# Six second-layer accumulations of a gated mix kernel split into two row tiles of 64 rows

## The chip, the cores and the metric

The kernel runs on one core of a Trainium2 chip. Its engines are TensorE (PE: matrix products, with weight loads shown apart as PEld), VectorE (DVE), ScalarE (ACT), GpSimd (POOL) and SyncE (SP, which here issues nearly all DMAs). Each engine runs its own instructions strictly in the order in which the program lists them, and waits for others through semaphores. The metric is the device time of one execution in microseconds, the median of several runs.

## What is computed

Two branches are mixed with a gate. Branch A is a short causal filter on `k`, a product with `v`, a long causal convolution over 2048 positions and a product with `q`. Branch B is a two-layer perceptron on the same `q`. Cut to what matters:

```python
x = A_q                                             # 2048 x 512
g = sigmoid((x * gate_w).sum(-1, keepdims=True))
k_shift = sum(k_pad[:, t:t + S] * shift_k[:, 3 - t] for t in range(4))
kv = k_shift * v
y = irfft(rfft(kv, 4096) * rfft(ssm_k, 4096))[:, :S] + kv * ssm_D
a = q * y
h = maximum(x @ w1, 0)                              # 2048 x 1792
b = h @ w2                                          # 2048 x 512
out = g * a + (1 - g) * b
```

## The kernel before

**Precision.** Every operand of the perceptron is split into a high and a low part of type fp32r (names ending in h and l, such as `hh` and `hl` for the hidden activations, `w1h` and `w1l` for the second layer's weights), and each product is made as three matmuls: high times high, high times low, low times high. That is three matmuls of 128 x 128 weights by 512 columns in place of one.

**Second layer.** `mlp2(era, c, s)` (lines 398 to 432) makes 128 rows of the second layer. The hidden dimension has 14 blocks of 128; an era is half of them (blocks 0 to 6, then 7 to 13). A chunk `c` is 512 positions, and `s` is one of its four groups of 128. So one accumulation is 7 blocks times 3 matmuls, 21 in all, into one bank of PSUM (`bank`, line 278; there are eight banks, and the planner counts them as "cv"). In era 0 the bank is then copied to a tile `y` by ACT (`keep`, lines 414 to 421); in era 1 DVE adds the bank to that tile (`plus`, line 429), or, in the last chunk, the final instruction reads the bank directly (`finish`, line 677). Chunk 3 comes first in era 1 and chunk 0 last.

**Convolution.** It runs in three stages beside the perceptron, with DRAM between them. Stage 1 (`stage1`, lines 451 to 471) is made of 16 units, named s1h and s1x in the profile: eight matmuls each on tiles of 32 rows x 64 columns, into four banks, copied out by ACT and stored. Stage 2 (`conv_mid`) begins when all of stage 1 is stored; its units are f_h and f_x (64 rows x 32 columns, line 575) and, two groups later, iv (32 x 64, line 652). Stage 3 begins when all of stage 2 is stored. It loads the result (`br`), and `conv_end` (lines 687 to 732) runs the cy matmuls (64 x 32, line 727) in two groups of four units, each unit of eight matmuls into two banks. `after` and `finish` then combine, on DVE, for each of the 16 output tiles: `t` from cy, the gate and q (line 737), in the last chunk also `t` plus the kept half of the second layer (line 740), and the output tile `o` (line 677), which SP stores.

**What sets the order.** Nothing is ordered by hand around the change. `Plan.order` (lines 97 to 232) is a list scheduler that runs when the program is built: every operation has an engine, a planned duration, a rank, dependencies, and buffers it takes and gives back. A stage-1 unit has `pair` set. It is placed only together with another one, right after an operation that carries `soon` (`twin`, lines 113 to 121), or alone when it has been waiting for over 50 planned microseconds (`LONG`, line 815). Before the change, the last block of every second-layer accumulation carries `soon`. Tile operations carry `tiles=True`, and the planner adds `SWITCH` at each change between tiles and full matmuls.

Of the kernel before, what the change touches and what calls it, by code (L numbers as in the profile page):

```python
# [11 lines left out]
OP = mybir.AluOpType  # L12

S, D, DFF = 2048, 512, 1792
# [52 lines left out]
def _flat(r):  # L67
    for x in r if isinstance(r, tuple) else (r,):
        yield from _flat(x) if isinstance(x, tuple) else (x,)


class Plan:
# [5 lines left out]
    def add(self, eng, dur, rank, fn, deps=(), take=(), give=(), dma=0, fifo=(), tiles=False, port=False, alt=None, pair=0, soon=False, ends=False):  # L78
        rank = tuple(_flat(rank))
        op = dict(tiles=tiles, alt=alt, port=port or eng == "POOL" and not dma, eng=eng, dur=dur, rank=rank, fn=fn, take=tuple(take), give=tuple(give), dma=dma, fifo=tuple(fifo),  # L80
                  pair=pair, soon=soon, ends=ends or soon, wait=0, next=[], asked=0.0, n=len(self.ops), rest=(), member=False)
        op["fn"] = fn if alt is None else lambda: fn(op["eng"])
        for d in deps:
            if d is not None:
                d["next"].append(op)
                op["wait"] += 1
        for q in fifo:
            self.turn.setdefault(q, []).append(op["n"])
        self.ops.append(op)
        return op  # L90
# [144 lines left out]
def act_time(n, psum=False):  # L235
    return n * 0.000833 + (0.05 if psum else 0.093)


def dve_time(n):
    return n * 0.001042 + 0.12  # L240


MM = 0.227
# [5 lines left out]
def build(tc, wf, xp, qn, kn, vn, hn, dn, sh, gw, w1, w2, cs1, ccf, cci, cib, out):  # L249
    nc = tc.nc  # L250
# [18 lines left out]
    add = plan.add  # L269
    T = {}  # L270
    cpool = [None, None]

    def tile_of(key, tag, w=D, dt=F32, bufs=None, rows=P, p=None):
        nm = tag + "_" + "_".join(map(str, key[1:] if len(key) > 1 else key))
        T[key] = (p or cpool[0]).tile([rows, w], dt, tag=tag, bufs=bufs or room.get(tag, 1), name=nm)
        return T[key]

    def bank(key, tag="cv"):
        T[key] = pm.tile([P, D], F32, tag=tag, bufs=room0[tag], name="_".join(map(str, key)))
        return T[key]  # L280
# [3 lines left out]
    mm = nc.tensor.matmul  # L284
# [6 lines left out]
    xdone, wdone, xhigh = {}, {}, {}  # L291
    ERAS = [range(0, NF // 2), range(NF // 2, NF)]
    CHUNKS = [list(range(NCHUNK)), list(range(NCHUNK))[::-1]]
# [56 lines left out]
    hdone, m1last, m2 = {}, {}, {}  # L350
    ydone, ystore = {}, {}
    at = [0]
# [45 lines left out]
    def mlp2(era, c, s):  # L398
        at[0] += 1
        prev = None  # L400
        fs = ERAS[era]
        z = slice(s * P, (s + 1) * P)
        for f in fs:
            def go(f=f):
                ps = bank(("m2", era, c, s)) if f == fs[0] else T["m2", era, c, s]
                mm(ps, T["hh", era, c, f][:, z], T["w", "h", 1, f], start=f == fs[0], stop=False)  # L406
                mm(ps, T["hh", era, c, f][:, z], T["w", "l", 1, f], start=False, stop=False)  # L407
                mm(ps, T["hl", era, c, f][:, z], T["w", "h", 1, f], start=False, stop=f == fs[-1])  # L408

            prev = add("PE", 3 * MM, (1, at[0], f), go, [hdone[era, c, f], wdone[1, f], prev], ["cv"] if f == fs[0] else (),  # L410
                       (["hh"] if s == 3 else []) + (["w2"] if s == 3 and c == CHUNKS[era][-1] else []), soon=f == fs[-1])
        n, i = 4 * c + s, at[0]
        if era == 0:
            def keep():
                if c:
                    tile_of(("y", n), f"y{n}", p=mp)
                else:
                    if s % 2 == 0:
                        tile_of(("y2", n), "yr", 2 * D, p=mp)
                    T["y", n] = T["y2", n - s % 2][:, s % 2 * D:(s % 2 + 1) * D]  # L420
                nc.scalar.copy(T["y", n], T["m2", era, c, s])

            two = ["yr"] if c == 0 and s % 2 == 0 else []
            ydone[n] = add("ACT", act_time(D, True), (0, -900 + i), keep, [prev], two, ["cv"], fifo=two)
            if c == 0:
                ystore[n] = add("SP", ISSUE, -20 + s, lambda: nc.sync.dma_start(yd[:, n], T["y", n]), [ydone[n], ystore.get(n - s % 2)], (), ["yr"] if s % 2 else [], dma=ROW)
        elif c != CHUNKS[1][-1]:
            def plus():
                nc.vector.tensor_tensor(T["y", n], T["m2", era, c, s], T["y", n], op=OP.add)

            ydone[n] = add("DVE", dve_time(D), (0, -900 + i), plus, [prev, ydone[n]], (), ["cv"])
        m2[era, c, s] = prev
# [322 lines left out]
    w = add("PE", WARM * 2 * MM / 2, (-3,), warm, (), ["cv"], ["cv"])  # L755
# [10 lines left out]
    for era in range(2):  # L766
        for n, c in enumerate(CHUNKS[era]):
            if era == 0 and c == NCHUNK - 1:
                for i in range(2):
                    for f in ERAS[1]:  # L770
                        load_w(i, f, -50 + f + 10 * i)
            for f in ERAS[era]:
                if era == n == 0 and f < G:
                    if f == 0:
                        mlp1_first()
                    continue
                give = ["x"] * 4 if f == ERAS[era][-1] and not (era == 0 and c == NCHUNK - 1) else []
                if era == 0 and c == NCHUNK - 1 and f >= G - 1:
                    give += ["w1"] * (4 if f == G - 1 else 1)
                mlp1(era, c, f, give)  # L780
            if n + 1 < NCHUNK:
                for k in range(4):
                    load_x(era, CHUNKS[era][n + 1], k, -40)
            for s in range(4):
                mlp2(era, c, s)
# [105 lines left out]
```

## Time and profile before

| what | value |
|---|---|
| median of 3 runs | 385.6 us (385.55 to 386.24) |
| the profiled execution | 385.97 us |
| its span, first to last instruction | 384.2 us |
| PE busy | 99% of the span |
| DVE busy | 69% |
| ACT, POOL busy | 34%, 24% |
| granted TensorE clock | 0.999 |

The profile is one execution. Its own time is 1.8 us over its span; the median of the runs is 1.4 us over that span. A timeline row gives the start in us from the span's start, the duration in us, the engine, the line and operation, the tiles (output, then inputs, numbers left out) with the tile of the array in use (rows*columns), and a count where rows are merged; in brackets stands the idle time before it and what ended it. Matmuls overlap: a matmul is shown longer than the distance to the next one, so the distance between starts is what one costs.

### The profile page before, as it was taken

To read this page: it belongs to the slowest core of one execution; us is meant where nothing else is said; L and a number is where in the kernel's file an instruction comes from. 1 tells how busy PE (TensorE), PEld (TensorE's weight loads), DVE (VectorE), ACT (ScalarE), POOL (GpSimd) and SP (SyncE) were. 2 spreads that over 40 slices of the span, in tenths; PEclk is the share of its full clock that TensorE was granted. 3 is DMA by queue.
4 is the path that set the end of the run, shared out by engine and by line. 5 is a ranking of instruction groups with operands and counts; after the bars stand their busy time and mean duration, and the time that the engine had idled before them with its cause. 6 is when DMAs were issued, how large, how long until landed. Compare 5 with 4: busy or idle time off the path is not lost.

```text
span 384.2 us, 6567 instructions
## 1 busy us (share of the span) xinstructions
PE 379.8 (99%) x2505; PEld 273.8 (71%) x2505; DVE 266.7 (69%) x356; ACT 128.8 (34%) x242; POOL 91.5 (24%) x77
## 2 busy tenths in 40 slices
PE   9999999999999999999999999999999999999996
PEld 5888788668877788788655765565587788688684
DVE  4698999797989028114799687897872347687691
ACT  5643524573147525533224022313400333012100
POOL 0000000000000000000199968866995001000000
PEclk9999999999999999999999999999999999999999
DMA  7997893898648763589867876686460798399331
GB/s 274 368 317 255 298 351 113 293 333 323 208 121 330 295 234 109 185 296 275 285 203 238 307 265 227 241 308 232 139 204 3 241 342 320 120 325 357 117 124 56
DMA packets 43474, 92.51 MB, mean 241 GB/s; under 512 B 4625, under 2 KB 7201, under 8 KB 43442
## 3 DMA queue, kind: packets, MB, share of 16 engines
q1 hardware_dynamic: 43090, 91.77, 68.8%
q8 instruction: 20, 0.33, 0.4%
q10 hardware_dynamic: 288, 0.26, 0.2%
q14 instruction: 12, 0.10, 0.1%
q0 software_dynamic: 64, 0.05, 0.0%
HBM read 61.66 MB, written 30.41 MB: 240 GB/s over the span
## 4 chain that ended last, share of the span: by engine, by line
PE 99%; DVE 0%; DVEq 0%; issue 0%
PE m L406 14%; PE m L407 13%; PE m L408 13%; PE m L376 13%; PE m L377 12%; PE m L378 12%; PE iv L652 4%; PE f_h L575 4%; PE f_x L575 4%; PE m L362 3%; PE s1x L459 2%; PE s1h L459 2%; PE cy L727 2%; PE warm L753 1%; DVE o L677 0%; DVEq L887 0%
## 5 line engine op out<-in xcount | busy, mean ns | idle before, releaser
L623 POOL TENSOR_TENSOR p<-p,ha 128x512 f32<-128x512 f32 x32 | 41.1, 1308 | 202.2 <-DVE ha L617 201.6
L406 PE MATMUL m<-w1h_h,hh 128*128 128x512 f32 x224 | 88.7, 396 | 0.0
L407 PE MATMUL m<-w1l_l,hh 128*128 128x512 f32 x224 | 87.3, 390 | 0.0
L408 PE MATMUL m<-w1h_h,hl 128*128 128x512 f32 x224 | 87.2, 389 | 0.0
L389 ACT ACTIVATE hh<-m 128x512 fp32r<-128x512 f32 x56 | 33.1, 598 | 126.4 <-PE m L378 122.1
L392 DVE SCALAR_TENSOR_TENSOR hl<-m,hh 128x512 fp32r<-128x512 f32 x56 | 38.3, 688 | 44.5 <-ACT hh L389 44.3
L376 PE MATMUL m<-xh_h,w0h_h 128*128 128x512 f32 x160 | 63.0, 394 | 0.0
L377 PE MATMUL m<-xl_l,w0h_h 128*128 128x512 f32 x160 | 62.3, 390 | 0.0
L378 PE MATMUL m<-xh_h,w0l_l 128*128 128x512 f32 x160 | 62.3, 389 | 0.0
L406 PEld LDWEIGHTS m<-w1h_h,hh 128*128 128x128 f32 x224 | 42.0, 188 | 19.1 <-ACT ev L464 6.5
L408 PEld LDWEIGHTS m<-w1h_h,hl 128*128 128x128 f32 x224 | 42.0, 188 | 9.0
L407 PEld LDWEIGHTS m<-w1l_l,hh 128*128 128x128 f32 x224 | 42.1, 188 | 8.3
L376 PEld LDWEIGHTS m<-xh_h,w0h_h 128*128 128x128 f32 x160 | 30.0, 188 | 11.1 <-issue 4.2
L378 PEld LDWEIGHTS m<-xh_h,w0l_l 128*128 128x128 f32 x160 | 30.0, 188 | 6.4
L377 PEld LDWEIGHTS m<-xl_l,w0h_h 128*128 128x128 f32 x160 | 30.0, 188 | 6.0
L518 DVE TENSOR_TENSOR acc<-acc,tmp 128x1024 f32<-128x1024 f32 x24 | 29.3, 1222 | 0.6
L302 DVE TENSOR_TENSOR w1l_l<-raw,w1h_h 128x512 fp32r<-128x512 f32 x14 | 9.4, 686 | 17.7 <-ACT w1h_h L299 17.7
L662 ACT COPY bv<-iv 128x512 f32<-128x512 f32 x16 | 8.7, 589 | 37.1 <-PE iv L652 31.9
L515 DVE TENSOR_TENSOR tmp<-in,sht_sht 128x512 f32<-128x512 f32 x32 | 20.8, 685 | 0.1
L623 POOL TENSOR_TENSOR p<-p,qa 128x512 f32<-128x512 f32 x16 | 20.7, 1317 | 0.0
L617 DVE TENSOR_TENSOR ha<-f_x,ha 128x1024 f32<-128x1024 f32 x16 | 19.5, 1221 | 1.3 <-DVE qb L617 0.5
L623 POOL TENSOR_TENSOR p<-p,qb 128x512 f32<-128x512 f32 x16 | 20.3, 1290 | 0.0
(72 smaller groups left out, 468.1 us busy)
## 6 DMA issues: line engine op xcount, KB each, us to landing
sa<-ev SPq DMA_DIRECT2D x64, 256.0 KB, 3.0
sb<-bv SPq DMA_DIRECT2D x32, 256.0 KB, 3.4
br<-sb SPq DMA_DIRECT2D x16, 512.0 KB, 6.8
raw<-xp SPq DMA_DIRECT2D x28, 256.0 KB, 4.2
raw<-w SPq DMA_DIRECT2D x24, 256.0 KB, 3.8
r_x<-sa SPq DMA_DIRECT2D x12, 512.0 KB, 5.1
in<-kn SPq DMA_DIRECT2D x10, 512.0 KB, 5.0
r_h<-sa SPq DMA_DIRECT2D x10, 512.0 KB, 6.3
```

The source lines that it names most:

```text
L376: mm(ps, part("h", f, k), T["x", "h", xe, c, k], start=k == 0, stop=False)
L377: mm(ps, part("h", f, k), T["x", "l", xe, c, k], start=False, stop=False)
L378: mm(ps, part("l", f, k), T["x", "h", xe, c, k], start=False, stop=k == 3)
L389: nc.scalar.activation(tile_of(("hh", era, c, f), "hh", dt=F32R, p=mp, bufs=HB), T["m1", era, c, f], AF.Relu)
L392: nc.vector.scalar_tensor_tensor(tile_of(("hl", era, c, f), "hl", dt=F32R, p=mp, bufs=HB), T["m1", era, c, f], 0.0, T["hh", era, c, f].bit ...
L406: mm(ps, T["hh", era, c, f][:, z], T["w", "h", 1, f], start=f == fs[0], stop=False)
L407: mm(ps, T["hh", era, c, f][:, z], T["w", "l", 1, f], start=False, stop=False)
L408: mm(ps, T["hl", era, c, f][:, z], T["w", "h", 1, f], start=False, stop=f == fs[-1])
L515: nc.vector.tensor_tensor(o[:, z], T["k", c + (j == 0) + part][:, u], T["sht",][:, j * D:(j + 1) * D], op=OP.mult)
L518: nc.vector.tensor_tensor(T["acc", c], T["acc", c], T[dst], op=OP.add)
L575: mm(ps[b][32 * j:32 * j + 32, :], T[k("cf")][at, 64 * j + 32 * o:64 * j + 32 * o + 32], T[k("r", t, j // 2)][at, (j % 2) * D:(j % 2 + 1) ...
L623: nc.gpsimd.tensor_tensor(planes("p", dst, n), planes("p", dst, n), planes(src, u, n), op=OP.add if sign > 0 else OP.subtract)
```

## The change

In six accumulations (era 0, chunks 1 and 2, `s` of 0, 1 and 2), each of the 21 matmuls becomes two: one over rows 0 to 63 of the operands, one over rows 64 to 127. The two go to different row tiles of the array, and each has a bank of its own. ACT copies the first bank to `y` as before, and a new DVE instruction (`both`) adds the second bank to `y`. The planned duration of a block stays at three matmuls; the first block takes two banks; and the last block of such an accumulation no longer carries `soon`.

```diff
@@ mlp2
         fs = ERAS[era]
+        wide = era == 0 and c in (1, 2) and s < 3
         z = slice(s * P, (s + 1) * P)
         for f in fs:
             def go(f=f):
+                if wide:
+
+                    for i in range(2):
+                        ps = bank(("m2", era, c, s, i)) if f == fs[0] else T["m2", era, c, s, i]
+                        T["m2", era, c, s, i] = ps
+                    for n, (a, b) in enumerate((("hh", "h"), ("hh", "l"), ("hl", "h"))):
+                        for i in range(2):
+                            r = slice(64 * i, 64 * i + 64)
+                            mm(T["m2", era, c, s, i], T[a, era, c, f][r, z], T["w", b, 1, f][r, :], start=f == fs[0] and n == 0, stop=f == fs[-1] and n == 2)
+                    return
                 ps = bank(("m2", era, c, s)) if f == fs[0] else T["m2", era, c, s]
...
-            prev = add("PE", 3 * MM, (1, at[0], f), go, [hdone[era, c, f], wdone[1, f], prev], ["cv"] if f == fs[0] else (),
-                       (["hh"] if s == 3 else []) + (["w2"] if s == 3 and c == CHUNKS[era][-1] else []), soon=f == fs[-1])
+            prev = add("PE", 3 * MM, (1, at[0], f), go, [hdone[era, c, f], wdone[1, f], prev], ["cv"] * (1 + wide) if f == fs[0] else (),
+                       (["hh"] if s == 3 else []) + (["w2"] if s == 3 and c == CHUNKS[era][-1] else []), soon=f == fs[-1] and not wide)
...
-                nc.scalar.copy(T["y", n], T["m2", era, c, s])
+                nc.scalar.copy(T["y", n], T["m2", era, c, s, 0] if wide else T["m2", era, c, s])
+
+            def both():
+                nc.vector.tensor_tensor(T["y", n], T["m2", era, c, s, 1], T["y", n], op=OP.add)
...
             ydone[n] = add("ACT", act_time(D, True), (0, -900 + i), keep, [prev], two, ["cv"], fifo=two)
+            if wide:
+                ydone[n] = add("DVE", dve_time(D), (0, -900 + i), both, [ydone[n]], (), ["cv"])
```

The order of the whole program follows from the planner, so the change moves more than the six accumulations. In the rows below, a name such as m_0_2_0 is the bank of era 0, chunk 2, group 0 (a fourth number is the row tile), hh_2_1 the hidden activations of chunk 2, block 1, and w1h_h_1 the weights of block 1. From the changed lines on, line numbers are 11 higher in `mlp2`'s old matmuls (406 to 408 become 417 to 419) and 16 higher behind it (stage 1's 459 becomes 475, cy's 727 becomes 743, 677 becomes 693, 709 becomes 725, 714 becomes 730, 737 becomes 753, 740 becomes 756). The row-tile matmuls stand on line 414.

PE, in chunk 2's second-layer accumulations, before: two stage-1 units stand side by side at the boundary between two accumulations.

```order
L408 MATMUL m_0_2_0_1133<-w1h_h_6_353,hl_2_6_1151 128x512
L459 MATMUL s1x_0_1181<-acc_791,s1c_s1t 64x512 x2
L459 MATMUL s1x_1_1184<-acc_791,s1c_s1t 64x512 x2
L459 MATMUL s1x_2_1187<-acc_791,s1c_s1t 64x512 x2
L459 MATMUL s1x_3_1190<-acc_791,s1c_s1t 64x512 x2
L459 MATMUL s1h_0_1198<-in_681,s1c_s1t 64x512 x2
L459 MATMUL s1h_1_1201<-in_681,s1c_s1t 64x512 x2
L459 MATMUL s1h_2_1204<-in_681,s1c_s1t 64x512 x2
L459 MATMUL s1h_3_1207<-in_681,s1c_s1t 64x512 x2
L406 MATMUL m_0_2_1_1219<-w1h_h_0_237,hh_2_0_1006 128x512
```

PE at the same accumulation now: a single unit stands between two blocks of a split accumulation.

```order
L414 MATMUL m_0_2_0_0_1073<-w1h_h_1_244,hl_2_1_983 128x512
L414 MATMUL m_0_2_0_1_1074<-w1h_h_1_244,hl_2_1_983 128x512
L475 MATMUL s1h_0_1096<-in_573,s1c_s1t 64x512 x2
L475 MATMUL s1h_1_1099<-in_573,s1c_s1t 64x512 x2
L475 MATMUL s1h_2_1102<-in_573,s1c_s1t 64x512 x2
L475 MATMUL s1h_3_1105<-in_573,s1c_s1t 64x512 x2
L414 MATMUL m_0_2_0_0_1073<-w1h_h_2_277,hh_2_2_993 128x512
L414 MATMUL m_0_2_0_1_1074<-w1h_h_2_277,hh_2_2_993 128x512
```

Stage 1 is visited eight times by PE before, always for two units; now it is visited ten times, six times for two units and four times for one, the four inside split accumulations of chunk 2. The last two units stood right behind the accumulation m_0_3_0 and now stand behind m_0_3_2, two accumulations later.

PE at the second group of cy (the last tile work of the program), before:

```order
L406 MATMUL m_1_0_0_3650<-w1h_h_9_1741,hh_0_9_3549 128x512
L407 MATMUL m_1_0_0_3650<-w1l_l_9_1750,hh_0_9_3549 128x512
L408 MATMUL m_1_0_0_3650<-w1h_h_9_1741,hl_0_9_3560 128x512
L727 MATMUL cy_3666<-br_3393,ibt_ibt 32x512
L727 MATMUL cy_3667<-br_3393,ibt_ibt 32x512
```

PE at the same place now:

```order
L417 MATMUL m_1_0_2_3838<-w1h_h_7_1847,hh_0_7_3544 128x512
L418 MATMUL m_1_0_2_3838<-w1l_l_7_1858,hh_0_7_3544 128x512
L419 MATMUL m_1_0_2_3838<-w1h_h_7_1847,hl_0_7_3549 128x512
L743 MATMUL cy_3842<-br_3577,ibt_ibt 32x512
L743 MATMUL cy_3843<-br_3577,ibt_ibt 32x512
```

The group stood behind the third of seven blocks of m_1_0_0; now it stands behind the first block of m_1_0_2. Before, 75 full matmuls follow it to the end of the program (12 of m_1_0_0 and 21 each of the three accumulations behind it); now 39 follow (18 of m_1_0_2 and 21 of m_1_0_3).

DVE at its end, before:

```order
L677 SCALAR_TENSOR_TENSOR o_3783<-m_1_0_1_3734,gs_3628,t_3754 128x512
L714 TENSOR_SCALAR gs_3769<-gs_3769 128x1
L737 SCALAR_TENSOR_TENSOR t_3790<-cy_3700,gs_3769,q_3648 128x512
L740 SCALAR_TENSOR_TENSOR t_3790<-yr_2959,gs_3769,t_3790 128x512
L714 TENSOR_SCALAR gs_3776<-gs_3776 128x1
L737 SCALAR_TENSOR_TENSOR t_3801<-cy_3701,gs_3776,q_3659 128x512
L740 SCALAR_TENSOR_TENSOR t_3801<-yr_2959,gs_3776,t_3801 128x512
L677 SCALAR_TENSOR_TENSOR o_3814<-m_1_0_2_3772,gs_3769,t_3790 128x512
L677 SCALAR_TENSOR_TENSOR o_3835<-m_1_0_3_3810,gs_3776,t_3801 128x256 x2
```

DVE at its end now:

```order
L730 TENSOR_SCALAR gs_3938<-gs_3938 128x1
L753 SCALAR_TENSOR_TENSOR t_3957<-cy_3886,gs_3938,q_3828 128x512
L756 SCALAR_TENSOR_TENSOR t_3957<-yr_3136,gs_3938,t_3957 128x512
L693 SCALAR_TENSOR_TENSOR o_3966<-m_1_0_2_3838,gs_3938,t_3957 128x512
L730 TENSOR_SCALAR gs_3945<-gs_3945 128x1
L753 SCALAR_TENSOR_TENSOR t_3969<-cy_3887,gs_3945,q_3836 128x512
L756 SCALAR_TENSOR_TENSOR t_3969<-yr_3136,gs_3945,t_3969 128x512
L693 SCALAR_TENSOR_TENSOR o_3973<-m_1_0_3_3929,gs_3945,t_3969 128x256 x2
```

From the first t of this cy group to the last o, DVE has the same set of instructions in both programs (eight t, four of line 740, eight o with the last one in two halves, two gate sums and two small gate instructions); only the o of m_1_0_2 moved ahead of the last t. Elsewhere DVE gains eight instructions: the six adds and two low-part subtractions that were POOL's.

## The prediction

> **What bounds the kernel now.** I read the busy shares first, then the chain that ended last.
>
> ```profile
> PE 379.8 (99%) x2505; PEld 273.8 (71%) x2505; DVE 266.7 (69%) x356; ACT 128.8 (34%) x242; POOL 91.5 (24%) x77
> PE 99%; DVE 0%; DVEq 0%; issue 0%
> ```
>
> PE is busy through 99% of the span, and the chain of waits runs over PE for 99%. So every nanosecond that PE gains or loses reaches the end one to one, until another engine takes over. Where could that happen? At the end of the program, so I read the timeline there next, DVE above all.
>
> ```profile
> 359.64 3.66 PE L727 MATMUL cy<-br,ibt_ibt 64*32 64x512 f32 x64
> 360.82 0.75 DVE L737 SCALAR_TENSOR_TENSOR t<-cy,gs,q 128x512 f32<-128x512 f32 x1 [1.73 <-PE cy L727]
> 361.81 0.15 PEld L727 LDWEIGHTS cy<-br,ibt_ibt 64*32 64x32 f32 x8 [0.28 <-DVE t L737]
> 363.73 1.41 DVE L737 SCALAR_TENSOR_TENSOR t<-cy,gs,q 128x512 f32<-128x512 f32 x2
> 365.05 0.74 DVE L677 SCALAR_TENSOR_TENSOR o<-y,gs,t 128x512 f32<-128x512 f32 x1
> 365.71 0.75 DVE L737 SCALAR_TENSOR_TENSOR t<-cy,gs,q 128x512 f32<-128x512 f32 x1
> 374.11 0.75 DVE L740 SCALAR_TENSOR_TENSOR t<-yr,gs,t 128x512 f32<-128x512 f32 x1
> 375.85 0.75 DVE L677 SCALAR_TENSOR_TENSOR o<-m,gs,t 128x512 f32<-128x512 f32 x1 [0.99 <-PE m L408]
> 380.61 0.88 DVE L677 SCALAR_TENSOR_TENSOR o<-m,gs,t 128x256 f32<-128x256 f32 x2 [4.01 <-PE m L408]
> ```
>
> The reader is to see a reserve. The last group of cy starts at 359.64 us. The first t starts 1.18 us later, and from there DVE works without a pause up to the end of the row at 374.11, that is to 374.86: 14.04 us. Then it waits for PE twice, 0.99 and 4.01 us. So at the end PE is the later of the two, but only by these 5 us. Whatever places the last cy later in PE's order uses this reserve up, and beyond it DVE sets the end. After the last o (380.61 + 0.88 = 381.49) 2.71 us of the 384.2 us span remain for the store and the end of the program.
>
> **The change part by part.**
>
> *1. The matmuls themselves.* What does one cost in the stream? The durations overlap, so I take starts: 36 steps from the first to the second row.
>
> ```profile
> 149.67 0.39 PE L378 MATMUL m<-xh_h,w0l_l 128*128 128x512 f32 x1
> 157.83 0.39 PE L408 MATMUL m<-w1h_h,hl 128*128 128x512 f32 x1
> ```
>
> 8.16 / 36 = 0.2267 us each. The change turns 6 x 21 = 126 of them into 126 pairs of half height. The trace has no tile of 64 rows x 128 columns, and no fp32r matmul on a tile. The nearest rows are the tiles of stage 2, in the chain of waits:
>
> ```profile
> 249.53 1.72 PE f_x L575 x32
> 251.25 0.43 PE m L376
> ```
>
> Here 32 matmuls on tiles of 64 rows, in two banks, take 1.72 us: 0.43 us for each set of eight, though one alone is shown with 0.59 us below.
>
> ```profile
> L575 PE MATMUL f_x<-r_x,cf 64*32 64x512 f32 x192 | 11.5, 589 | 0.0
> L727 PE MATMUL cy<-br,ibt_ibt 64*32 64x512 f32 x128 | 7.3, 592 | 0.0
> ```
>
> So tiles run beside each other, also with different halves of the rows into different banks, and a pair should cost what one full matmul does. The bounds are these. From below: an f32 matmul is issued as two passes (the profile counts 128 cy matmuls, the program has 64), and a set's 0.43 us is 0.215 us for half of it, which may be the price of 512 columns without an extra; a pair would then cost 0.012 us less than now, 126 x 0.012 = 1.5 us in all. From above: no overlap at all, 126 x 0.2267 = 28.6 us more. I take 0.2267 us, no change, since type, columns and length of the weight load stay those of the full matmul.
>
> *2. Changes between tilings.* One stage-1 visit:
>
> ```profile
> 158.15 1.11 PE L459 MATMUL s1x<-acc,s1c_s1t 32*64 32x512 f32 x16
> 159.06 1.06 PE L459 MATMUL s1h<-in,s1c_s1t 32*64 32x512 f32 x16
> 160.05 0.50 PE L406 MATMUL m<-w1h_h,hh 128*128 128x512 f32 x1
> 160.39 0.39 PE L407 MATMUL m<-w1l_l,hh 128*128 128x512 f32 x1
> 160.85 0.40 PE L406 MATMUL m<-w1h_h,hh 128*128 128x512 f32 x1
> ```
>
> From 157.83 to 160.85 are 3.02 us. Four full matmuls (4 x 0.2267 = 0.91) and four sets (4 x 0.43 = 1.72) account for 2.63; the visit's entry and exit cost 0.39. By the order, stage 1 is visited ten times in place of eight: 2 x 0.39 = 0.78. The split accumulations themselves stand in two stretches (chunk 1's three, chunk 2's three), each entered from and left for full matmuls. Their price is bounded by 0 (the columns stay 128 wide) and a visit's 0.39 plus what their longer load shows:
>
> ```profile
> L406 PEld LDWEIGHTS m<-w1h_h,hh 128*128 128x128 f32 x224 | 42.0, 188 | 19.1 <-ACT ev L464 6.5 <-issue 4.2
> L459 PEld LDWEIGHTS s1h<-in,s1c_s1t 32*64 32x64 f32 x128 | 3.8, 131 | 3.1 <-issue 2.1
> ```
>
> 188 - 131 = 0.06 us more: 0.45. I take the upper, since each change between tilings in the trace costs something: 0.90. Together 1.68 us.
>
> *3. Six adds on DVE, and two subtractions from POOL.* The add has the form of era 1's:
>
> ```profile
> L429 DVE TENSOR_TENSOR y<-m,y 128x512 f32<-128x512 f32 x12 | 8.2, 686 | 11.7 <-PE m L408 11.7
> 62.00:158.00 96.00, 96.00 (x560) 72.52 (x558) 68.02 (x82) 46.48 (x87) 0.00 (x0) 1.00 0.68 239
> ```
>
> Eight times 0.69 is 5.5 us of DVE. In the stretch in which they fall (62 to 158 us: PE 96.00 busy, then weight loads 72.52, DVE 68.02, ACT 46.48, POOL 0) DVE has 28 us free, so they are hidden and cost nothing. If the cover failed, they would cost 5.5 us at most. What queues behind a waiting add on DVE is the low part hl of a later block and the filter's products for stage 1. PE needs the first soon, the second only much later, since stage 1's units are placed later than before. The bank of an add is freed one ACT copy (0.59 us) and one add later than now; with two banks per accumulation and four for a stage-1 unit, six of eight are in use, so I count no wait.
>
> *4. The last cy moves back.* By the order, 75 full matmuls followed the last group of cy and 39 do now: 36 more stand ahead of it, 36 x 0.2267 = 8.16 us. All tile work stands ahead of its end in both. So the group starts at 359.64 + 8.16 + 1.68 = 369.48 us. This costs PE nothing in itself; it uses the reserve.
>
> *5. The end.* DVE's first t comes at 369.48 + 1.18 = 370.66. The same 24 instructions follow, 14.04 us, and between them the o of m_1_0_2, which costs a step of 0.66 us (365.05 to 365.71): 385.36. The last two halves take 0.88, the store and the end 2.71: 388.95 us. Is PE later? Now three second-layer accumulations hold banks during cy, so the fourth unit needs the banks of the second and third t. The third t ends 4.84 us after the group's start (363.73 + 0.75 less 359.64); 0.28 more until the load, 0.86 for two sets, 0.43 for the first full matmul and 38 x 0.2267 = 8.61 for the rest give 15.0, and 0.39 until the last is done: 15.4 us. DVE reaches its last o at 1.18 + 14.04 + 0.66 = 15.9. DVE is later, by 0.5 us; PE's bank wait is covered by this.
>
> **Sum.** 388.95 against a span of 384.2: +4.75 us. The profiled execution took 385.97 us, the median is 385.6. Put on the median: 385.6 + 4.75 = 390.35, so about 390.4 us, 1.2% slower.
>
> **The rivals.**
>
> *Cheaper pairs.* The 0.012 us by which a full matmul exceeds half a set might go on a half-height tile: the sets of eight speak for it, the same type and width against it. 126 x 0.012 = 1.5 us less: 388.9 us. Chance 0.24. The Trainium skill, "TensorE: Matmul & The Clock Gate", section "Back-to-back issue gap", gives 512 columns / 2.4 GHz + 2.5 ns, about 216 ns; by that this rival would come out, but the trace's full matmuls take 227 ns, so the rule does not hold for these even unsplit.
>
> *Loads in the open.* A pair needs two weight loads of 128 columns (0.19 us each in the row above) in the time of one. If the second is not hidden behind the running pair, each pair costs what the first matmul after a visit costs, whose load is in the open: 160.39 - 160.05 = 0.34 us. That is 126 x 0.113 = 14.3 us more, 404.7 us. Against it, 32 half-height tile matmuls with as many loads, if shorter ones, in 1.72 us. Chance 0.07. The Trainium skill, same page, Part 3, "Measured speedup vs the span model", gives four row tiles at 512 columns a speedup of 3.07 only; by that an estimate for a pair is 0.2267 x 4 / 3.07 = 0.295 us, and for the time 399 us. Stage 2's rows show no such loss.
>
> *No overlap.* The change doesn't do what it says; the pairs run one after the other: 390.4 + 28.6 = 419 us. Chance 0.05.
>
> *Waits ahead.* A bank or operand comes late in the denser stretch of chunk 2 or at cy, by one or two DVE instructions of 0.75 us: 391.1 to 391.9. Chance 0.07.
>
> *PE alone sets the end: no slower.* If DVE's 14.04 us could be shortened by over 3 us (its gate sums and small gate instructions done earlier, its t's not held), the later cy would cost nothing; only 1.68 us of tiling changes remain, and with cheaper pairs 0.2: 385.8 us. It decides where DVE is done before PE's 39 matmuls, 3.6 + 0.3 + 8.8 = 12.7 us after the group's start, against 15.9. The order keeps the gate sums between the t's, so I give it 0.05: 0.03 within 0.2%, 0.02 faster by more.
>
> **How the numbers follow.** My forecast itself has 0.52. The range reaches from 388.1 (cheaper pairs, and stretches entered free: 390.4 - 1.5 - 0.8) to 392.6 (waits ahead, 391.9, and one more step of 0.66 in DVE's chain). It leaves out loads in the open, no overlap and the case on the other side, 0.17 in all. About 0.2% (0.8 us) is what a measurement of this kernel can tell from no change. Faster 0.02, within it 0.03, slower 0.95.
>
> **What would show it.** Part 1: starts of successive pairs on line 414 should be 0.227 us apart; 0.215 is the first rival, 0.34 or 0.45 the next two. Part 2: stage-1 visits of 0.39. Part 4: the last cy starts near 369.5 us. Part 5: the chain of waits ends on DVE, with no idle time of DVE before the last o, and PE has a pause between units of cy, ended by DVE's t. A cy group at 361 us, or DVE idle for PE at the end, would prove me wrong.

## The result, and the profile after

The changed kernel takes 391.94 us (median of 4 runs, 391.35 to 392.29) against 385.81 us before: a ratio of 1.0156, 95% interval [1.0139, 1.0174]. That is 6.1 us slower; 390.4 us was predicted, with a range of 388.1 to 392.6. The profiled execution took 391.35 us, with a span of 389.5 us against 384.2.

The profile's page of the changed kernel, busy shares and the chain that ended last:

```profile
PE 383.2 (98%) x2631; PEld 272.7 (70%) x2631; DVE 270.0 (69%) x364; ACT 127.9 (33%) x242; POOL 88.2 (23%) x75
PE 95%; DVE 3%; issue 1%; DVEq 0%
```

The chain no longer runs over PE to the end: DVE has 3% of it, and 1% is issue time between DVE's instructions. The timeline shows where the chain changes engines, first PE around the last group of cy (start and duration in us; a count where rows are merged):

```profile
369.40 0.39 PE L419 MATMUL m<-w1h_h,hl 128*128 128x512 f32 x1
369.72 3.07 PE L743 MATMUL cy<-br,ibt_ibt 64*32 64x512 f32 x48
373.16 1.04 PE L743 MATMUL cy<-br,ibt_ibt 64*32 64x512 f32 x2 [0.36 <-DVE t L753]
374.61 1.09 PE L743 MATMUL cy<-br,ibt_ibt 64*32 64x512 f32 x14 [0.41 <-DVE t L753]
375.62 0.50 PE L417 MATMUL m<-w1h_h,hh 128*128 128x512 f32 x1
...
384.38 0.39 PE L419 MATMUL m<-w1h_h,hl 128*128 128x512 f32 x1
```

The kernel before, behind its group (which starts at 359.64) and at its last matmul:

```profile
363.24 0.50 PE L406 MATMUL m<-w1h_h,hh 128*128 128x512 f32 x1
...
380.18 0.39 PE L408 MATMUL m<-w1h_h,hl 128*128 128x512 f32 x1
```

The group now starts at 369.72 us, 10.08 us later than before, and lasts 5.90 us to the next full matmul (375.62) in place of 3.60. These 2.30 us more are a wait: the fourth unit waits for banks that DVE's t instructions free. Then DVE, from the first t of the group to the last o:

```profile
370.90 0.75 DVE L753 SCALAR_TENSOR_TENSOR t<-cy,gs,q 128x512 f32<-128x512 f32 x1 [5.36 <-PE cy L743]
...
373.81 1.41 DVE L753 SCALAR_TENSOR_TENSOR t<-cy,gs,q 128x512 f32<-128x512 f32 x2
...
380.53 0.68 DVE L725 CUSTOM_DVE_ANT_0 j<-q,gwt_gwt 128x512 f32<-128x512 f32 x1
...
381.94 0.74 DVE L753 SCALAR_TENSOR_TENSOR t<-cy,gs,q 128x512 f32<-128x512 f32 x1
382.72 0.75 DVE L756 SCALAR_TENSOR_TENSOR t<-yr,gs,t 128x512 f32<-128x512 f32 x1
383.56 0.75 DVE L693 SCALAR_TENSOR_TENSOR o<-m,gs,t 128x512 f32<-128x512 f32 x1
...
385.06 0.75 DVE L756 SCALAR_TENSOR_TENSOR t<-yr,gs,t 128x512 f32<-128x512 f32 x1
385.90 0.88 DVE L693 SCALAR_TENSOR_TENSOR o<-m,gs,t 128x256 f32<-128x256 f32 x2
```

No row after the first carries a wait, here or among the rows left out, though the kernel before waited 0.99 and 4.01 us for PE at this place. DVE works from 370.90 to 386.78 without a wait. Before, the last o started 0.43 us after the start of PE's last matmul (380.61 and 380.18). PE's last matmul now starts at 384.38, so the last o could start at 384.8; DVE comes to it at 385.90. So DVE is the later one, by 1.1 us.

The 5.3 us by which the span grew are thus 1.9 us ahead of cy (10.08 less 8.16 for the 36 matmuls that moved ahead of it), 2.3 us of PE's wait inside cy, and 1.1 us by which DVE is later than PE.

The split work itself, at the start of chunk 1's stretch and at its end:

```profile
63.72 0.39 PE L378 MATMUL m<-xh_h,w0l_l 128*128 128x512 f32 x1
64.03 0.50 PE L414 MATMUL m<-w1h_h,hh 64*128 64x512 f32 x2
64.37 0.40 PE L414 MATMUL m<-w1l_l,hh 64*128 64x512 f32 x2
64.60 0.40 PE L414 MATMUL m<-w1h_h,hl 64*128 64x512 f32 x2
...
76.88 0.39 PE L414 MATMUL m<-w1h_h,hl 64*128 64x512 f32 x2
...
78.24 0.39 PE L414 MATMUL m<-w1h_h,hl 64*128 64x512 f32 x2
78.56 0.50 PE L417 MATMUL m<-w1h_h,hh 128*128 128x512 f32 x1
78.90 0.40 PE L418 MATMUL m<-w1l_l,hh 128*128 128x512 f32 x1
```

A row of x2 is one pair. From 76.88 to 78.24 are six steps, 0.227 us each: a pair of half-height matmuls takes what a full one took. At the entry two steps are longer (0.31 and 0.34), at the exit as well (0.32 and 0.34): each change of tiling costs some 0.2 us more than the matmuls themselves.

### The profile page after: what moved, and what is told of

It reads as the page before. It is cut to its first block, busy times and chain, and to the rows that moved or that the text cites. A ratio compares the mean times of both kernels' runs of the same rounds, so it can differ in the third digit from the quotient of the medians.

```text
span 389.5 us, 6829 instructions
## 1 busy us (share of the span) xinstructions
PE 383.2 (98%) x2631; PEld 272.7 (70%) x2631; DVE 270.0 (69%) x364; ACT 127.9 (33%) x242; POOL 88.2 (23%) x75
## 4 chain that ended last, share of the span: by engine, by line
PE 95%; DVE 3%; issue 1%; DVEq 0%
PE m L376 13%; PE m L377 12%; PE m L378 12%; PE m L417 10%; PE m L419 10%; PE m L418 10%; PE m L414 8%; PE iv L668 4%; PE f_h L591 4%; PE f_x L591 4%; PE m L362 3%; PE s1x L475 2%; PE s1h L475 2%; PE cy L743 1%; DVE o L693 1%; PE warm L769 1%
## 5 line engine op out<-in xcount | busy, mean ns | idle before, releaser
L417 PE MATMUL m<-w1h_h,hh 128*128 128x512 f32 x182 | 72.3, 397 | 0.0
L418 PE MATMUL m<-w1l_l,hh 128*128 128x512 f32 x182 | 70.9, 390 | 0.0
L419 PE MATMUL m<-w1h_h,hl 128*128 128x512 f32 x182 | 70.9, 390 | 0.0
L417 PEld LDWEIGHTS m<-w1h_h,hh 128*128 128x128 f32 x182 | 34.1, 188 | 15.7 <-issue 4.9
L419 PEld LDWEIGHTS m<-w1h_h,hl 128*128 128x128 f32 x182 | 34.2, 188 | 7.3
L418 PEld LDWEIGHTS m<-w1l_l,hh 128*128 128x128 f32 x182 | 34.2, 188 | 6.7
```

## The experiments

Two theories stood against each other. **The order costs it:** the splits move the last cy back until DVE's reserve is gone, and a split costs only the changes between tilings. **The splits cost it:** pairs, second banks and adds. In each case the ratio is to the kernel before on the same chip.

**The changed kernel again**, as a reference for the others. It shared a chip with the six other splits, the order without splits and the cy held back to 39 matmuls. The other experiments ran on two further chips, on which the kernel before took 386.0 and 385.74 us in place of 386.08; where they are set against the 391.57 us here, the chips differ.

> The changed kernel once more, beside the others on one chip. Every theory: 391.9 us, 6.1 above the kernel before.

Measured: 391.57 us, ratio 1.0141 [1.0128, 1.0155].

**Six other splits, with cy left where it was.**

```diff
-        wide = era == 0 and c in (1, 2) and s < 3
+        wide = era == 0 and (c, s) in ((0, 0), (0, 1), (0, 2), (3, 1), (3, 2), (3, 3))
```

> Six accumulations are split as in the change, but others: chunk 0's groups 0 to 2 and chunk 3's groups 1 to 3. With these the planner leaves every tile unit where it stood before (eight stage-1 visits, 75 full matmuls behind the last cy); the split work stands in two stretches. Theory 'the order costs it' (the last cy moves back and uses up DVE's reserve; a split itself costs only the changes between tilings): two stretches x 0.44 us, so 385.8 + 0.9 = 386.7 us. Rival 'the split accumulations cost it' (1 us each, as pairs, second banks or adds): 391.9 us.

Measured: 386.57 us, ratio 1.0013 [1.0004, 1.0022]. The order is not quite the old one that was expected: by the profile three of the eight stage-1 visits stand one accumulation later (they start at 43.65, 125.72 and 132.61 us, against 38.27, 120.34 and 127.46 before). The last visit and both cy groups stand where they stood. The timeline at the end of this kernel:

```profile
360.49 1.09 PE L743 MATMUL cy<-br,ibt_ibt 64*32 64x512 f32 x16
381.46 0.88 DVE L693 SCALAR_TENSOR_TENSOR o<-m,gs,t 128x256 f32<-128x256 f32 x2 [4.01 <-PE m L419]
```

The cy group starts 0.85 us later than before (two stretches), and DVE again waits 4.01 us for PE. Six splits with six adds cost 0.5 us by the median; the other 5.0 us of the change's loss on this chip (391.57 against 386.57) are not theirs.

**The same six-split test in four stretches.**

```diff
-        wide = era == 0 and c in (1, 2) and s < 3
+        wide = era == 0 and (c, s) in ((0, 0), (0, 1), (0, 2), (1, 2), (2, 2), (3, 3))
```

> As the first experiment with the old order, but the six splits are chunk 0's groups 0 to 2, group 2 of chunks 1 and 2, and group 3 of chunk 3, in four stretches. If a stretch is what a split costs: 4 x 0.44 = 1.8 us, 387.6 us. If it is the split accumulations or their adds: as much as with two stretches.

Measured: 387.77 us, ratio 1.0048 [1.0035, 1.0060]. Here too three of the eight stage-1 visits stand one accumulation later, while the last one and cy stand where they stood. Six splits in both, but 1.8 us (387.77 against 386.0 before) where the stretches are four, and 0.5 where they are two: what is paid goes by the stretches and not by the splits. So it is their entry and exit.

**The change's order without splits.** All rows of the order stay, but full matmuls stand in place of the pairs.

```diff
-                if wide:
-
-                    for i in range(2):
...
-                    return
...
-                nc.scalar.copy(T["y", n], T["m2", era, c, s, 0] if wide else T["m2", era, c, s])
+                nc.scalar.copy(T["y", n], T["m2", era, c, s])
...
-                nc.vector.tensor_tensor(T["y", n], T["m2", era, c, s, 1], T["y", n], op=OP.add)
+                pass
```

> The planner sees the changed kernel, so the order is that of the change, but the six accumulations are made with full matmuls into one bank and the six adds are left out. Theory 'the order costs it': all of the change's loss but the two stretches' entries and exits (0.9 us) and a little at four visits stays: 390.9 us. Rival 'the splits cost it': 385.8 us, or 386.6 with two more stage-1 visits.

Measured: 391.02 us, ratio 1.0126 [1.0113, 1.0140]. The timeline at its cy group, behind it and at the last o:

```profile
369.15 3.07 PE L733 MATMUL cy<-br,ibt_ibt 64*32 64x512 f32 x48
...
375.05 0.50 PE L407 MATMUL m<-w1h_h,hh 128*128 128x512 f32 x1
...
385.35 0.88 DVE L683 SCALAR_TENSOR_TENSOR o<-m,gs,t 128x256 f32<-128x256 f32 x2
```

Without a single split, 4.9 us of the loss are still there: cy lasts 5.90 us again, and the last o waits for no engine. Together with the six other splits this settles between the two theories: the order costs it.

**The last cy alone, late.** In the kernel before, the last cy group is made to wait for one more block (`m2b` holds each block's operation).

```diff
-        deps = [ibload] + [r[0] for r in ready.values()]
+        deps = [ibload] + [r[0] for r in ready.values()] + ([m2b[1, 0, 2, 7]] if LAST in ns else [])
```

> The kernel before, with the last cy group alone held back until the first block of m_1_0_2 is done, so that 39 full matmuls follow it in place of 75. No split, no added visit. DVE has its two late gate sums ahead of this cy group here, so its chain is about 1.5 us shorter than in the changed kernel. Theory 'a late cy uses up the reserve': cy starts at 359.6 + 8.2 = 367.8 us, PE pauses for DVE's t before the fourth unit as in the changed kernel, and the end follows PE by then: 15.1 us to the last o, 0.9 and 2.7 behind it, 386.5 us of span, 388.1 us in time (up to 389 if DVE still is the later one). Rival 'each microsecond of delay costs': 394.0 us. Rival 'PE is always the bound': 385.8 us.

Measured: 388.26 us, ratio 1.0055 [1.0042, 1.0067]. The timeline of this kernel:

```profile
367.53 3.07 PE L728 MATMUL cy<-br,ibt_ibt 64*32 64x512 f32 x48
...
372.42 1.09 PE L728 MATMUL cy<-br,ibt_ibt 64*32 64x512 f32 x14 [0.41 <-DVE t L738]
373.43 0.50 PE L406 MATMUL m<-w1h_h,hh 128*128 128x512 f32 x1
...
382.61 0.88 DVE L678 SCALAR_TENSOR_TENSOR o<-m,gs,t 128x256 f32<-128x256 f32 x2 [0.33 <-PE m L408]
```

The group starts 7.9 us later than before, and the time grows by 2.2 only: some 5.7 us of the delay are absorbed. With DVE's two gate sums ahead of cy, PE is again the later one at the end, by 0.33 us. What PE lost is the wait for banks inside cy: the group lasts 5.90 us (367.53 to 373.43), as in the change, in place of 3.60, and these 2.30 us are the whole loss. So a late cy costs something even where DVE does not set the end.

The smaller delay, with `m2b[1, 0, 0, 13]` in the same line, so that 63 matmuls follow:

> The kernel before, with the last cy group alone held back until the last block of m_1_0_0 is done: 63 full matmuls follow it, 12 fewer than before. It starts 2.7 us later. Theory 'a reserve of 5 us': the delay is within it, no change, 385.8 us. Rival 'each microsecond of delay costs': 388.5 us.

Measured: 385.70 us, ratio 0.9997 [0.9988, 1.0006]. The timeline:

```profile
361.96 3.66 PE L728 MATMUL cy<-br,ibt_ibt 64*32 64x512 f32 x64
365.56 0.50 PE L406 MATMUL m<-w1h_h,hh 128*128 128x512 f32 x1
...
380.21 0.88 DVE L678 SCALAR_TENSOR_TENSOR o<-m,gs,t 128x256 f32<-128x256 f32 x2 [3.68 <-PE m L408]
```

2.3 us of delay cost nothing: the group lasts 3.60 us as before, so no unit of it waits longer for a bank, and DVE still waits 3.68 us for PE at the end. (Here too the two gate sums stand ahead of cy, so DVE's chain is lighter by some 1.5 us than before.) So the price of a late cy has a threshold, between 2.3 and 7.9 us of delay in these two kernels.

**DVE's last chain made lighter.**

```diff
-                nc.vector.scalar_tensor_tensor(T["o", n][:, z], T[key][:, z], T["gs", n][:, 2:3], T["t", n][:, z], op0=OP.mult, op1=OP.add)
+                if n // 4 != 1:
+                    nc.vector.scalar_tensor_tensor(T["o", n][:, z], T[key][:, z], T["gs", n][:, 2:3], T["t", n][:, z], op0=OP.mult, op1=OP.add)
```

> The changed kernel, with the four o instructions of chunk 1 left out (t is stored in place of o, so chunk 1 of the output is without its second-layer part). All four stand in DVE's last chain and cost 0.66 us a step, 2.7 us. Theory 'DVE sets the end': DVE is done 2.7 us earlier, PE's fourth cy unit gets its banks 1.4 us earlier, and PE's last matmul, which has 1.1 us in hand now, just precedes DVE's last o: 389.4 us. Rival 'PE or the stores set the end': 391.9 us.

Measured: 388.99 us, ratio 1.0076 [1.0062, 1.0089]. Taking 2.7 us of work from DVE takes 2.6 us from the time of the changed kernel. The timeline:

```profile
370.00 4.39 PE L744 MATMUL cy<-br,ibt_ibt 64*32 64x512 f32 x64
374.32 0.50 PE L417 MATMUL m<-w1h_h,hh 128*128 128x512 f32 x1
...
383.54 0.88 DVE L694 SCALAR_TENSOR_TENSOR o<-m,gs,t 128x256 f32<-128x256 f32 x2 [0.22 <-PE m L419]
```

From cy's start to the last o are 13.54 us (16.18 in the change), and PE has just become the later one. PE gained too: its cy group lasts 4.32 us (370.00 to 374.32) in place of 5.90, since the t's that free its banks come sooner.

The other half of the question is how far PE is behind. Here the last two tiles take the gate of two others:

```diff
-            def gate_sum(k=k):
+            def gate_sum(k=k, n=n):
+                if n in (LAST - 1, LAST):
+                    T["gs", n] = T["gs", n - 2]
+                    return
```

> The changed kernel, with the gate of the last two output tiles (groups 2 and 3 of chunk 0) left out: they use the gate of groups 0 and 1. This takes the two gate sums and two small gate instructions out of DVE's last chain, 1.47 us; the t's before them, which free cy's banks, stay where they are. Theory 'DVE sets the end by 1.1 us, PE is next': DVE reaches its last o at 384.4 us, PE's last matmul is done for it at 384.8, so the gain is cut off at 1.1 us: 390.5 us. Rival 'DVE sets the end with room to spare': 390.1 us. Rival 'gate sums are beside the path': 391.6 us.

Measured: 390.77 us, ratio 1.0122 [1.0105, 1.0139]. By the time alone this is inconclusive, since the interval overlaps that of the changed kernel. The timeline decides:

```profile
370.39 3.07 PE L746 MATMUL cy<-br,ibt_ibt 64*32 64x512 f32 x48
...
385.47 0.88 DVE L693 SCALAR_TENSOR_TENSOR o<-m,gs,t 128x256 f32<-128x256 f32 x2 [0.45 <-PE m L419]
```

From cy's start to the last o are 15.08 us, 1.10 less than in the change, though 1.47 us of work went. The gain is cut off where PE becomes the later one, which confirms the 1.1 us.

**The change's own splits with an earlier cy.**

```diff
-LONG = 50.0, 50.0, 12.0, 0.0
+LONG = 30.0, 30.0, 12.0, 0.0
```

> The changed kernel with the same six splits, but a stage-1 unit may stand alone after 30 planned us in place of 50. Stage 1 then has 14 visits (8 before, 10 in the change), two of them inside split work, and 75 full matmuls stand behind the last cy again. Theory 'the late cy costs most': DVE's reserve is back and only changes between tilings are paid: 6 x 0.40 + 2 x 0.44 = 3.3 us, 389.1 us. Rival 'splits and visits cost it': at least the change's 391.9 plus four more visits, 393.5 us.

Measured: 389.71 us, ratio 1.0093 [1.0080, 1.0107]. The timeline:

```profile
363.11 3.66 PE L743 MATMUL cy<-br,ibt_ibt 64*32 64x512 f32 x64
366.71 0.50 PE L417 MATMUL m<-w1h_h,hh 128*128 128x512 f32 x1
...
384.08 0.88 DVE L693 SCALAR_TENSOR_TENSOR o<-m,gs,t 128x256 f32<-128x256 f32 x2 [4.01 <-PE m L419]
```

The same six splits, six stage-1 visits more than before, and still 1.9 us faster than the change, because 75 matmuls follow the last cy again: the group lasts 3.60 us, and DVE waits its 4.01 us for PE. The expected 389.1 was 0.6 too low: the added visits cost a little more than 0.40 us each. No version here beats the kernel before.

## Why the prediction was right

**Part 1, the pairs at 0.227 us: right.** The six steps above give 0.227 us, and rows rounded to 0.01 us leave some 0.002 open; 0.215 lies outside. The rivals "cheaper pairs", "loads in the open" and "no overlap" fall with the rows above.

**Part 2, changes between tilings, 1.68 us: right in kind, somewhat small.** Counted from the first second-layer matmul, which stands ahead of the change (23.90 us before, 23.73 now), cy starts 10.25 us later. Less the 8.16 of the matmuls, 2.09 us are left for tilings, 0.4 more than the sum took. (The 10.08 above is smaller, as this execution was 0.17 us ahead at that point.) In the order without splits cy starts 9.24 us later by the same count (369.15 less 24.17): 1.08 us for the two more visits, where 0.78 was taken, which leaves 1.01 for the two stretches, where 0.90 was taken. The two experiments with cy where it was give 0.5 us for two stretches (0.15 to 0.85 by the interval; 0.85 by cy's start) and 1.8 for four, where 0.45 each was taken. A stage-1 visit inside split work costs a little more than the 0.39 taken, and it is for one unit only:

```profile
106.00 0.40 PE L414 MATMUL m<-w1h_h,hl 64*128 64x512 f32 x2
106.33 1.11 PE L475 MATMUL s1h<-in,s1c_s1t 32*64 32x512 f32 x16
107.38 0.50 PE L414 MATMUL m<-w1h_h,hh 64*128 64x512 f32 x2
...
108.88 0.39 PE L414 MATMUL m<-w1h_h,hh 64*128 64x512 f32 x2
```

From 106.00 to 108.88 are 2.88 us; seven pairs (1.59) and the unit's two sets of eight (0.86) account for 2.45, so the visit costs 0.43.

**Part 3, the adds hidden: right.** Six of them stand in the experiment with six other splits too, whose whole cost is that of its stretches. In the changed kernel PE is busy for all of the 96 us from 62 to 158, in which the adds fall.

**Part 4, cy 36 matmuls later: right.** Its start was put at 369.48 us; it is 369.72. That this "costs PE nothing in itself" holds for the matmuls that changed places; the bank wait inside cy, which part 5 worked out, cost PE 2.30 us.

**Part 5, DVE sets the end: right**, by 1.1 us where 0.5 was worked out. From the first t to the last o DVE took 15.00 us against 14.70: some steps between dependent neighbours are longer in this order (382.72 to 383.56 for line 756 and the o behind it, 0.84, where 0.66 was taken for the added o). The o of m_1_0_1 has moved as well, ahead of the two gate sums. PE was ready for the last o 15.1 us after cy's start, 0.3 sooner than worked out. PE's bank wait, which the prediction called covered, is so only because DVE is later still: without those last 1.1 us of DVE the span would be 4.2 us longer than before, and 2.3 of them are this wait. It stands in no term of the sum, as the sum goes over DVE, but it is the larger part of what the late cy costs.

**The size.** The span grew by 5.3 us against 4.75 in the sum, 0.24 at cy's start and 0.30 in DVE's chain: both were taken too small, so the misses added up. The median grew by 6.1, as the profiled execution is the fastest of the four here and was slower than the median before (385.97 against 385.81). Executions of the same order differ by up to 0.6 us in their first 38 us, ahead of all that the change touches. The first stage-1 unit in the changed kernel, and in the one without two gate sums, whose order is the same up to there:

```profile
38.10 0.68 PE L475 MATMUL s1h<-in,s1c_s1t 32*64 32x512 f32 x8
```

```profile
38.73 0.69 PE L475 MATMUL s1h<-in,s1c_s1t 32*64 32x512 f32 x8
```

From there to the cy group both take the same 331.6 to 331.7 us. So part of the miss against the median is this scatter; in the second comparison, of 391.57 us, the loss was 5.5 us.

**What in the change moves the order.** The planner is a part of the kernel, so its order can be had without the chip. By its rule (`twin`) a pair of stage-1 units may follow an accumulation only when that carries `soon`, and when seven of the eight banks are free or about to be. The change touches both: it drops `soon`, and it holds a second bank until the add is done. Each alone moves the order. With two banks and `soon` kept the planner gives the order of the change; with one bank and `soon` dropped it gives ten visits and 39 matmuls behind the last cy again. Only with one bank and `soon` kept do the eight visits and the 75 matmuls come back. The added DVE instruction is not needed for it: left out of the plan, the order of PE stays that of the change. These are orders of the planner; no run measured them apart.

## What to carry to other kernels

Splitting a full matmul into two row tiles costs nothing by itself here, and gains nothing; what it costs is the entry and exit of a stretch, and what a second bank or a dropped flag does to a scheduler. Where one engine is busy for 99% of the span, look for the engine that follows it at the end: its reserve there (5 us here) says how late the last producer may come before the follower sets the end. Look also at the buffers which the follower frees: here the producer itself waited 2.3 us for banks. Taking DVE work from between the freeing t's gave 1.6 of them back; taking it from behind them gave none. To tell an order's cost from an operation's, run the new order with the old operations, and the new operations where the old order survives.

## What was not expected

Two weight loads of half height run beside each other and beside the pair. Their group in the changed kernel (count, busy us, mean ns, idle time before):

```profile
L414 PEld LDWEIGHTS m<-w1l_l,hh 64*128 64x128 f32 x84 | 7.9, 184 | 1.5
```

Each is shown with 184 ns, hardly less than the 188 ns of a full one. One after the other the 84 loads would take 15.5 us, but they keep the engine busy for 7.9 only: they overlap two by two, and so two fit into each step of 227 ns. And the 227 ns are not a matter of height: tiles of half height take them too.
